# First block of x in four loads of two heads from two queues, in a fused attention and two-layer kernel

## The chip, the cores and the metric

The kernel runs on one core of a Trainium2 chip. The metric is the device time of one execution in microseconds. Engines: PE (TensorE), VectorE (DVE), ScalarE (ACT), GpSimd (POOL) and SyncE (SP). SP, ScalarE and POOL each issue DMAs to a queue of their own; the loads that change the type go through POOL's.

## The reference

```
x: (8, 8, 512, 64) f32 = B, H, S, D     state: (8, 8, 32, 64) f32
a     = softmax(x @ state^T / 8)        xread = a  @ state
a2    = softmax(state @ x^T / 8)        sread = a2 @ x
y     = concat([xread, sread], axis=2), heads side by side: (4352, 512)
h     = y @ w_in                        (512, 2048)
out   = (max(h, 0) + alpha * min(h, 0)) @ w_out      (2048, 512), out (4352, 512) f32
```

## The kernel before

The eight batches are blocks of 512 rows each; a ninth block holds the 256 rows of `sread`. `w_in` is applied to the states first (`state_w_in`, tiles `m`), so that a block's hidden rows come out of `m` and the softmax weights `aT` (`first`, step F, line 568). The ReLU-like function takes a ScalarE pass (`negative`, N) and a VectorE pass (`prelu`, G, line 624). The second layer is plain for block 0 (`second`, S, `second_out`, O) and uses sums and products of halves for the other blocks (U, P, K, Q).

The order of all work is written out by hand in the string `ORDER`: each token is a step with its arguments, and each engine runs its instructions in the order in which the tokens issue them. A letter `a`, `v` or `p` in a token names the engine (ScalarE, VectorE, POOL), a last digit on PE's steps the PSUM bank. The first tokens are

```
stc.0.a stt.0.1 sbd.0.a cx.0.0.v lst xt.0.0.0.2 cx.1.0.v sbd.1.a xt.0.1.0.3 xo.0.0.0.a tsc.0.0.4 xo.0.1.0.v tsc.1.0
cx.1.1.v Z.5.1 smax.0.0 xt.0.1.1.0 xo.0.1.1.v cx.0.1.a xt.0.0.1.2 ssh.v.0.0 sto.0.a Z.3.1 tsc.1.1.5 xo.0.0.1.a tsc.0.1
```

Before them stand the loads of x for block 0 (two, from SP's queue), of its states (64 KB, from ScalarE's queue), of alpha (four small ones, from SP's) and of the first part of `w_in` (POOL's), and nine filler matmuls (`fill`, Z, line 230) that keep PE going. Then:

- `stc` casts the first states (line 248), `stt` transposes them on PE (line 242), `sbd` copies them to `st_pairs` (line 262) and `sto` to `stT`.
- `cx.j.g` (`x0_cast`, line 175) casts to f16 one of two parts of x for the group `g` of four heads: before, all four heads, every other pair of rows (`j`).
- `xt.0.j.g` (`x_transposed`, line 300) transposes four 128x128 pieces of it on PE, `xo.0.j.g` (line 306) copies them to `xT`, `tsc.j.g` (`token_scores`, line 355) makes four score matmuls with `st_pairs`.
- `smax.0.g` (line 381), `ssh` (386), `sexp` (395), `ssum` (402, 403) and `snorm` (406) are the softmax of the first block in two halves, by group `g`; `at` and `ao` turn it into `aT`.
- `str`, `m`, `mo` prepare the other states and the tiles `m` (lines 242, 519, 543, 545).

The tile pool gives buffers by tag: the x tiles take the two of `ts` (4 KB a partition each), which the softmax tiles use afterwards. The tag `osb` has four of 2 KB, for rows of output.

Of the kernel before, what the change touches and what calls it, by code (L numbers as in the profile page):

```python
# [8 lines left out]
F32 = mybir.dt.float32  # L9
# [91 lines left out]
def kernel(  # L101
# [17 lines left out]
    nc = tc.nc  # L119

    B, H, S, D = x.shape
# [12 lines left out]
    att = ctx.enter_context(tc.tile_pool(name="att", bufs=2))  # L134
    moe = ctx.enter_context(tc.tile_pool(name="moe", bufs=2))
# [4 lines left out]
    def single(k, name, shape, dtype):  # L140
        return ps.tile(shape, dtype, name=name, tag=f"k{k}", bufs=1)
# [4 lines left out]
    def copier(e):  # L146
        return nc.scalar.copy if e == "a" else nc.vector.tensor_copy
# [4 lines left out]
    live = {}  # L152
    xgs = {}
    x0s = []
# [6 lines left out]
        )  # L161


    def load_x0(g):
        if g == 0:
            xgs["first"] = att.tile([128, H, 2, 2, D], F16, name="xg_first", tag="xg", bufs=3)
        t = att.tile([128, 4, 2, 2, D], F32, name=f"x0_{g}", tag="ts", bufs=2)
        x0s.append(t)
        nc.sync.dma_start(
            t.rearrange("p k j r d -> p k (j r d)"),  # L170
            x[0, 4 * g : 4 * g + 4].rearrange("k (p t) d -> p k (t d)", t=4),
        )

    def x0_cast(j, g, e):
        copier(e)(xgs["first"][:, 4 * g : 4 * g + 4, j, :, :], x0s[g][:, :, j, :, :])

    load_x0(0)
    load_x0(1)
    rows = state.rearrange("b h n d -> (b h n) d")
    n0 = H * N  # L180
    n_j = (B * H * N - n0) // 128
    st0_32 = consts.tile([128, 2, D], F32)
    nc.scalar.dma_start(st0_32, rows[:n0, :].rearrange("(g p) d -> p g d", p=128))
    alpha_rows = consts.tile([128, 32], F32)
    nc.vector.memset(alpha_rows, 0.0)
    alpha_quarters = moe_alpha.rearrange("(jc q c) -> q jc c", q=4, c=32)
# [28 lines left out]
    ident = consts.tile([128, 128], F16)  # L215
# [7 lines left out]
    st_pairs = consts.tile([128, H, 2, N], F16)  # L223
# [61 lines left out]
    def x_tile(b):  # L285
        if ("xT", b) not in live:
            live["xT", b] = att.tile([128, H, 2, 128], F16, name=f"xT_{b}", tag="xT", bufs=2)
        return live["xT", b]
# [7 lines left out]
    def x_transposed(b, j, g, k):  # L296
        b = b or "first"
        t = live["xp", b, j, g] = single(k, f"xT_ps{b}_{j}_{g}", [128, 4, 128], F16)
        for i in range(4):
            nc.tensor.transpose(  # L300
                t[:, i, :], xgs[b][:, 4 * g + i, j, :, :].rearrange("p r d -> p (r d)"), ident
            )

    def x_out(b, j, g, e):
        b = b or "first"
        copier(e)(x_tile(b)[:, 4 * g : 4 * g + 4, j, :], live.pop(("xp", b, j, g)))

    def scores(b, j=None):
        js = slice(0, 2) if j is None else slice(j, j + 1)
# [37 lines left out]
        soft_tiles(b)  # L347
        nc.vector.transpose(live["ts", b], live["sc", b].rearrange("p r j g s -> p (r j g s)"))

    def token_scores(j, g, k=None):  # L350
        if ("tsc", g) not in live:
            live["tsc", g] = single(k, f"tsc_{g}", [128, 2, 2, 4, N], F32)
        for k4 in range(4):
            h = 4 * g + (k4 ^ g)
            nc.tensor.matmul(
                live["tsc", g][:, j, :, k4, :],
                live["xT", "first"][:, h, j, :],
                st_pairs[:, h, :, :],
                start=True,
                stop=True,  # L360
                skip_group_check=True,
            )

    def tokens_transposed(j, k):
        t = live["at", j] = single(k, f"at_ps{j}", [128, 4, 128], F16)
# [386 lines left out]
    def quarter_out(b, th, dh, e=None):  # L752
# [12 lines left out]
        "stc": first_states_cast, "stt": first_states_transposed, "sto": first_states_out,  # L765
        "oma": one_less_alpha, "sbd": first_states_paired, "str": states_transposed, "sro": states_out,
        "xd": x_transposed_dma, "xt": x_transposed, "xo": x_out, "sc": scores, "cx": x0_cast, "tsc": token_scores,
        "at": tokens_transposed, "ao": tokens_out,
        "sb": score_blocks, "smax": state_max, "ssh": state_shift, "sexp": state_exp,
# [41 lines left out]
```

## Time and profile before

| | |
|---|---|
| median of 3 runs | 209.31 us (209.25 to 209.49) |
| profiled execution | 209.3 us, span of its instructions 207.2 us |
| PE busy | 198.9 us (96%) |
| VectorE busy | 182.6 us (88%) |
| ScalarE busy | 148.7 us (72%) |
| POOL busy | 144.0 us (70%) |
| granted TensorE clock | 1.000 |

Busy shares are means over the whole span. The start, the middle and the end of the kernel have different limits, so the stretch that a change touches is read by itself, in the timeline and in the chain of waits, which follows the work that ended last back to what released it.

### The profile page before, as it was taken

Reading aid. Unit: us, or ns where it says so; the run is one execution under the profiler, and the core shown is the slowest. Engines: PE = TensorE matmul, PEld = TensorE weight load, DVE = VectorE, ACT = ScalarE, POOL = GpSimd, SP = SyncE. Lnnn points to the kernel's source line nnn. Section 1 sums busy time; section 2 is a strip of 40 time slices with the busy share of each in tenths; the row PEclk is TensorE's granted clock in tenths of the full one; section 3 lists DMA queues with packets and bytes.
Section 4 is the critical chain, followed back from the end, with each engine's and each line's share of the span. In section 5 each row is a group of like instructions: output and inputs, shape, how many; then the busy total and the mean of one; then the engine's idle time right before and its main releaser. Section 6 shows DMA issues by size and latency. Waiting matters only on the chain.

```text
span 207.2 us, 5043 instructions
## 1 busy us (share of the span) xinstructions
PE 198.9 (96%) x2003; PEld 131.7 (64%) x2003; DVE 182.6 (88%) x277; ACT 148.7 (72%) x298; POOL 144.0 (70%) x87
## 2 busy tenths in 40 slices
PE   7789989999999999999999999999999999999992
PEld 2443433445666666677677766778767767888881
DVE  0899999999999999999999999998899988577650
ACT  3799998988789969988786899586677575321211
POOL 8173099999999999999897999949900697210100
PEclk9999999999999999999999999999999999999999
DMA  5999999949599999267979702112002021012134
GB/s 178 223 204 204 206 202 184 116 126 198 92 155 166 175 221 179 38 79 135 252 97 131 214 17 51 55 54 103 0 0 99 6 101 54 0 51 74 48 136 152
DMA packets 45943, 24.74 MB, mean 119 GB/s; under 512 B 24288, under 2 KB 45408, under 8 KB 45920
## 3 DMA queue, kind: packets, MB, share of 16 engines
q1 hardware_dynamic: 32960, 15.74, 31.2%
q0 software_dynamic: 12688, 8.62, 29.2%
q8 instruction: 15, 0.25, 0.5%
q10 hardware_dynamic: 272, 0.07, 0.1%
q14 instruction: 8, 0.07, 0.1%
HBM read 18.36 MB, written 8.91 MB: 132 GB/s over the span
## 4 chain that ended last, share of the span: by engine, by line
PE 81%; DVE 14%; issue 1%; DMA 1%; ACT 1%; POOL 0%; DVEq 0%; POOLq 0%; ACTq 0%
PE px L726 23%; PE h L568 23%; PE pv L726 12%; DVE g L624 7%; PE py L726 6%; PE o L638 6%; PE h L577 3%; PE m_ps L519 3%; PE fill L230 2%; DVE mx L381 1%; PE sr_ps L469 1%; DVE r L402 1%; DMA out_dram<-oq 1%; PE sc L316 1%; DVE ts L386 1%
## 5 line engine op out<-in xcount | busy, mean ns | idle before, releaser
L624 DVE SCALAR_TENSOR_TENSOR g<-neg,oma_sb,h 128x512 f16<-128x512 f32 (+1 forms) x144 | 94.5, 710 | 4.3 <-ACT neg L621 3.5
L621 ACT ACTIVATE neg<-h 128x512 f32<-128x512 f32 (+1 forms) x144 | 76.1, 590 | 14.0 <-PE h L568 8.2
L568 PE MATMUL h<-aT,m 128*128 128x512 f16 x256 | 64.5, 379 | 0.7 <-DVE g L624 0.5
L726 PEld LDWEIGHTS <-gsum 128*128 128x128 f16 x480 | 46.6, 98 | 9.6 <-issue 1.0
L568 PEld LDWEIGHTS <-m 128*128 128x128 f16 x256 | 24.1, 98 | 25.1 <-issue 4.3
L726 PEld LDWEIGHTS <-g 128*128 128x128 f16 x360 | 34.9, 98 | 7.3 <-issue 0.9
L705 POOL TENSOR_TENSOR gsum<-g 128x1024 f16<-128x1024 f16 (+1 forms) x14 | 28.7, 2060 | 14.4 <-PE pv L726 14.3
L705 POOL TENSOR_TENSOR gsum<-g,g 128x1024 f16<-128x1024 f16 x11 | 23.4, 2129 | 13.2 <-DVE g L624 13.1
L726 PE MATMUL px<-ws,gsum 128*128 128x256 f16 x240 | 29.8, 273 | 0.0
L742 ACT COPY kept<-px 128x512 f32<-128x512 f32 (+1 forms) x21 | 12.2, 582 | 23.8 <-PE px L726 22.8
L705 POOL TENSOR_TENSOR gsum<-gsum,g 128x1024 f16<-128x1024 f16 x11 | 23.4, 2126 | 3.4 <-DVE gsum L705 2.7
L705 POOL TENSOR_TENSOR gsum<-g,gsum 128x1024 f16<-128x1024 f16 x11 | 23.4, 2131 | 0.3
L545 ACT CAST m<-m_ps 128x512 f16<-128x512 f32 x36 | 19.9, 622 | 2.8 <-PE m_ps L519 2.7
L386 POOL TENSOR_TENSOR ts<-ts,mx 128x1024 f32<-128x1024 f32 x7 | 13.4, 1916 | 9.3 <-DVE mx L381 8.8
L638 PE MATMUL o<-w_out_sb,g 128*128 128x512 f16 x64 | 16.5, 379 | 0.0
L759 DVE TENSOR_TENSOR oq<-pv,kept 128x512 f32<-128x512 f32 (+1 forms) x16 | 10.5, 653 | 6.7 <-ACT kept L742 4.4
L726 PE MATMUL px<-w_out_sb,g 128*128 128x256 f16 x120 | 16.1, 273 | 0.0
L726 PE MATMUL px<-w_out_sb,gsum 128*128 128x256 f16 x120 | 16.1, 273 | 0.0
L726 PE MATMUL py<-w_out_sb,g 128*128 128x256 f16 x120 | 16.1, 273 | 0.0
L726 PE MATMUL pv<-ws,gsum 128*128 128x256 f16 x120 | 15.7, 273 | 0.0
L726 PE MATMUL pv<-ws,g 128*128 128x256 f16 x120 | 15.6, 273 | 0.0
L543 ACT CAST m<-m_ps 128x1024 f16<-128x1024 f32 x12 | 12.5, 1042 | 1.7 <-PE m_ps L519 1.6
(81 smaller groups left out, 232.7 us busy)
## 6 DMA issues: line engine op xcount, KB each, us to landing
out_dram<-oq SPq DMA_DIRECT2D x28, 256.0 KB, 2.6
xg<-in_x_dram POOLq DMA_DIRECT2D x8, 512.0 KB, 7.4
w_in_sb<-in_moe_w_in_dram POOLq DMA_DIRECT2D x4, 512.0 KB, 8.7
w_out_sb<-in_moe_w_out_dram POOLq DMA_DIRECT2D x4, 512.0 KB, 12.7
x<-in_x_dram SPq DMA_DIRECT2D x2, 512.0 KB, 4.9
out_dram<-osb SPq DMA_DIRECT2D x4, 256.0 KB, 4.3
out_dram<-oq SPq DMA_DIRECT2D x4, 128.0 KB, 2.1
st<-in_state_dram POOLq DMA_DIRECT2D x1, 224.0 KB, 7.3
```

Of the source, the lines that this page charges most:

```text
L386: engine(e).tensor_tensor(blocks(cols(live["ts", b], j, S)), blocks(scored(b, j)), over_blocks(cols(live["mx", b], j, S // N)), ALU.subtract,)
L519: nc.tensor.matmul(t[N * k : N * (k + 1), :], st_head(b, h)[64 * r : 64 * r + 64, :], w_in_sb[64 * r : 64 * r + 64, c, 512 * f : 512 * (f ...
L543: copier(e)(m_tile(b, f), t)
L545: copier(e)(m_tile(b, f)[:, g, :], t[g])
L568: nc.tensor.matmul(h.rearrange("p (r j s) -> p r j s", r=2, j=2), ms[b, f][:, g, 128 * j : 128 * (j + 1)], weights(b, g), start=(g == 0), ...
L621: nc.scalar.activation(neg, h, RELU, bias=0.0, scale=-1.0)
L624: nc.vector.scalar_tensor_tensor(g_tile(b, jc), negs.pop((b, jc)), oma_sb[:, jc : jc + 1], hs.pop((b, jc)), ALU.mult, ALU.add,)
L638: nc.tensor.matmul(outs[b, q], g_tile(b, jc)[:, 128 * q : 128 * (q + 1)], w_out_sb[:, jc, :], start=not begun and jc == 2 * jc2, stop=left ...
L705: engine(e).tensor_tensor(t, x(), y(), op)
L726: nc.tensor.matmul(pbanks[b, name][:, i, :], of(b, c)[:, j, 128 * i : 128 * (i + 1)], moving[:, 4 * c + j, :], start=not begun and j == 0, ...
L742: copier(e)(t, pbanks[b, "x"])
L759: nc.vector.tensor_tensor(osb, pbanks[b, name], kept[b, add], ALU.add)
```

## The change

Block 0 of x is loaded in four DMAs of two heads each (256 KB) instead of two of four heads (512 KB). Pairs 0 and 1 (heads 0 to 3) are issued from SP's queue, pairs 2 and 3 (heads 4 to 7) from ScalarE's, behind the first states. The steps keep their names, engines and places in `ORDER`, but their first number now picks a pair of heads of the group and not every other pair of rows: `cx.i.g` casts all rows of pair `i` of group `g`, `xt` transposes the four pieces of that pair, `xo` copies them, `tsc` makes its four score matmuls. The number and the size of casts, copies, transposes and matmuls stay the same. The tiles of the loads move from the tag `ts` to the tag `osb`.

```diff
-    def load_x0(g):
-        if g == 0:
+    def load_x0(pair, queue):
+        if pair == 0:
             xgs["first"] = att.tile([128, H, 2, 2, D], F16, name="xg_first", tag="xg", bufs=3)
-        t = att.tile([128, 4, 2, 2, D], F32, name=f"x0_{g}", tag="ts", bufs=2)
+        t = moe.tile([128, 2, 2, 2, D], F32, name=f"x0_{pair}", tag="osb", bufs=4)
         x0s.append(t)
-        nc.sync.dma_start(
+        queue.dma_start(
             t.rearrange("p k j r d -> p k (j r d)"),
-            x[0, 4 * g : 4 * g + 4].rearrange("k (p t) d -> p k (t d)", t=4),
+            x[0, 2 * pair : 2 * pair + 2].rearrange("k (p t) d -> p k (t d)", t=4),
         )
-    def x0_cast(j, g, e):
-        copier(e)(xgs["first"][:, 4 * g : 4 * g + 4, j, :, :], x0s[g][:, :, j, :, :])
-    load_x0(0)
-    load_x0(1)
+    def pair_of_heads(i, g):
+        return slice(4 * g + 2 * i, 4 * g + 2 * i + 2)
+    def x0_cast(i, g, e):
+        copier(e)(xgs["first"][:, pair_of_heads(i, g)], x0s[2 * g + i])
+    load_x0(0, nc.sync)
+    load_x0(1, nc.sync)
...
     nc.scalar.dma_start(st0_32, rows[:n0, :].rearrange("(g p) d -> p g d", p=128))
+    load_x0(2, nc.scalar)
+    load_x0(3, nc.scalar)
...
         for i in range(4):
-            nc.tensor.transpose(
-                t[:, i, :], xgs[b][:, 4 * g + i, j, :, :].rearrange("p r d -> p (r d)"), ident
-            )
+            if b == "first":
+                block = xgs[b][:, 4 * g + 2 * j + i // 2, i % 2, :, :]
+            else:
+                block = xgs[b][:, 4 * g + i, j, :, :]
+            nc.tensor.transpose(t[:, i, :], block.rearrange("p r d -> p (r d)"), ident)
...
-        copier(e)(x_tile(b)[:, 4 * g : 4 * g + 4, j, :], live.pop(("xp", b, j, g)))
+        t = live.pop(("xp", b, j, g))
+        if b == "first":
+            copier(e)(
+                x_tile(b)[:, pair_of_heads(j, g)].rearrange("p h j s -> p (h j) s"), t
+            )
+        else:
+            copier(e)(x_tile(b)[:, 4 * g : 4 * g + 4, j, :], t)
...
-    def token_scores(j, g, k=None):
+    def token_scores(i, g, k=None):
...
-        for k4 in range(4):
-            h = 4 * g + (k4 ^ g)
-            nc.tensor.matmul(
-                live["tsc", g][:, j, :, k4, :],
...
+        for h in range(8)[pair_of_heads(i, g)]:
+            for j in range(2):
+                nc.tensor.matmul(
+                    live["tsc", g][:, j, :, (h - 4 * g) ^ g, :],
```

More of the change, by code (lines that the diff above doesn't have):

```diff
@@ L348, in score_blocks @@
         nc.vector.transpose(live["ts", b], live["sc", b].rearrange("p r j g s -> p (r j g s)"))
-    def token_scores(j, g, k=None):
+    def token_scores(i, g, k=None):
         if ("tsc", g) not in live:
             live["tsc", g] = single(k, f"tsc_{g}", [128, 2, 2, 4, N], F32)
-        for k4 in range(4):
-            h = 4 * g + (k4 ^ g)
-            nc.tensor.matmul(
-                live["tsc", g][:, j, :, k4, :],
[L357 to L362, printed above, removed]
+        for h in range(8)[pair_of_heads(i, g)]:
+            for j in range(2):
+                nc.tensor.matmul(
+                    live["tsc", g][:, j, :, (h - 4 * g) ^ g, :],
+                    live["xT", "first"][:, h, j, :],
+                    st_pairs[:, h, :, :],
+                    start=True,
+                    stop=True,
+                    skip_group_check=True,
+                )
     def tokens_transposed(j, k):
```

## The prediction

> **What bounds the kernel now.** I began with the span and the clock, then busy time in three stretches (columns after the window: busy us of PE, PEld, DVE, ACT, POOL, then granted clock, DMA share, GB/s).
>
> ```profile
> core 0: 207.2 us, clock 1.000
> 7.70:15.60 7.90, 6.57 (x89) 3.46 (x89) 7.61 (x16) 6.78 (x13) 3.79 (x5) 1.00 1.25 205
> 15.60:30.00 14.40, 13.40 (x130) 5.58 (x129) 14.36 (x21) 14.38 (x28) 5.63 (x5) 1.00 1.31 204
> 30.00:200.00 170.00, 169.85 (x1730) 117.66 (x1729) 156.70 (x232) 122.83 (x251) 129.54 (x67) 1.00 0.52 103
> ```
>
> From 30 us on PE is busy 169.85 of 170.00 us: nothing in the change reaches that stretch, which only starts sooner or later. From 7.7 to 30 us VectorE is full (7.61 of 7.90, 14.36 of 14.40). The change lies ahead of that, so what it is worth is read at one instant: when VectorE begins its unbroken run. The chain of waits for the first 30 us says what sets that instant (start, length, what).
>
> ```profile
> 1.45 4.02 PE fill L230 x9
> 5.47 0.37 PE st_ps L242 x4
> 5.87 0.37 ACT st_pairs L262
> 6.25 0.37 ACT st_pairs L262
> 6.64 0.59 ACT xT_first L306
> 7.28 0.42 PE tsc L355 x8
> 7.72 0.69 DVE mx L381
> ```
>
> The run begins at 7.72 with the maximum over the first scores (step smax.0.0). Ahead of it stand nine filler matmuls, the transposes of the first states, three ScalarE copies in a row, and the scores. No cast of x and no landing of x is in this chain. The timeline of the first 13 us has the work around it (start, length, engine, line, what; in brackets the idle time before it and what ended it).
>
> ```profile
> 0.74 0.48 ACTq L183 DMA_DIRECT2D st<-in_state_dram  x1
> 0.74 1.02 SPq L169 DMA_DIRECT2D x<-in_x_dram  x2
> 1.25 1.28 ACT L248 ACT_TABLE_LOAD   x1 [1.25 <-PEq L795]
> 1.35 0.92 POOL L198 DMA_DIRECT2D w_in_sb<-in_moe_w_in_dram  x1
> 1.80 1.95 SPq L188 DMA_DIRECT2D alpha_rows<-in_moe_alpha_dram  x4
> 3.98 0.15 PEld L230 LDWEIGHTS <-pattern 128*128 128x128 f16 x1 [0.28 <-issue]
> 4.41 0.15 PEld L230 LDWEIGHTS <-pattern 128*128 128x128 f16 x1 [0.28 <-issue]
> 4.83 0.91 POOL L158 DMA_DIRECT2D xg<-in_x_dram  x1
> 4.88 0.30 ACT L248 CAST st<-st 128x128 f16<-128x128 f32 x1 [2.35 <-DMA st<-in_state_dram]
> 5.17 1.16 DVE L175 CAST xg_first<-x 128x512 f16<-128x512 f32 x2 [3.99 <-DMA x<-in_x_dram]
> 5.40 0.18 PEld L242 LDWEIGHTS <-st 128*64 128x64 f16 x4 [0.84 <-ACT st L248]
> 6.05 0.73 PE L300 MATMUL xT_psfirst<-ident,xg_first 128*128 128x128 f16 x8 [0.23 <-DVE xg_first L175]
> 6.81 0.42 DVE L306 COPY xT_first<-xT_psfirst 128x512 f16<-128x512 f16 x1 [0.49 <-PE xT_psfirst L300]
> 7.12 0.62 ACT L175 CAST xg_first<-x 128x512 f16<-128x512 f32 x1
> 7.16 0.42 DVE L175 CAST xg_first<-x 128x512 f16<-128x512 f32 x1
> 12.65 0.41 PE L519 MATMUL m_ps<-w_in_sb,stT 64*32 64x512 f16 x8 [0.79 <-DMA w_in_sb<-in_moe_w_in_dram]
> ```
>
> VectorE waits 3.99 us for x, but that is idle time before 7.72 that costs nothing: ScalarE's copy of the same half starts at 6.64, behind its two copies for st_pairs, when the transposed x has been there since about 6.5. Last, for the loads, the tile x (its casts and time from issue to landing), the line of the state's load, and DMA queues by window (packets, MB, share of 16 engines; q1 is SP's queue, q10 ScalarE's, q0 POOL's).
>
> ```profile
> L175 DVE CAST xg_first<-x x3: 407/417/828, 5.2 to 7.2; 128x512 f16<-128x512 f32 x3
> DMA to landing us min/median/max: 4.4/4.9/5.3
> DMA to landing us min/median/max: 4.1/4.1/4.1
> q1 hardware_dynamic: 444, 0.44, 73.7%
> q10 hardware_dynamic: 271, 0.07, 17.3%
> q1 hardware_dynamic: 269, 0.27, 109.5%
> q0 software_dynamic: 61, 0.06, 47.5%
> DMA packets 263, 0.21 MB, mean 206 GB/s; under 512 B 66, under 2 KB 263, under 8 KB 263
> q1 hardware_dynamic: 60, 0.12, 72.0%
> q0 software_dynamic: 66, 0.03, 48.8%
> ```
>
> The first landing row is x, the second the state. Then the windows: 2.7 to 4.4 us (q1, q10), 4.5 to 5.2 (q1, alone), 5.2 to 6 (q0's first packets), 6 to 7 (nearly all q0), 56 to 56.5 (q1 and q0 together). So x lands at 0.74+4.4 = 5.1 and at some 1.26+5.3 = 6.6, the state at 0.74+4.1 = 4.8. The second 512 KB takes 1.4 us, 0.7 us for 256 KB.
>
> **The change, part by part.**
>
> *When each pair lands.* The same 1 MB in the same 1 KB rows, so I keep the same total: the last pair lands when the last half does now, 6.6. Between, the queues share: from 2.7 to 4.4 us x and the state move side by side, 444 and 271 packets. Pair 0 has half the bytes of the present first load and lands first, 5.1-0.7 = 4.4. Pair 1 has two ends: 5.1, if pairs 2 and 3 take nothing from SP's queue, and 6.6, if all end together. I take it from the row of the state, which stands ahead of pair 2 on its queue: it lands 0.3 us before the first half of x; only from there on does pair 2 take turns, and pair 1's last 0.3 us doubles: 5.1+0.3 = 5.4. Pair 2 then follows at some 5.9, pair 3 at 6.6.
>
> *First half: casts, transposes, scores of heads 0 to 3.* The counts stay: four casts and four copies of 512 elements, 16 transposes, 16 score matmuls, at the durations above. VectorE casts pair 0 at 4.4 and pair 1 at 5.45. One cast took 828 ns against 407 to 417 for the others, at 5.17, inside POOL's DMA issue (4.83 to 5.74); so I charge 0.42 to 0.83 us, and pair 1 is cast by 5.9 to 6.3; now the second cast ends at 5.17+1.16 = 6.33. PE's transposes follow no later than now, and VectorE's copy stays at 6.81 or goes sooner. None of this moves smax.0.0, because ScalarE's copy still starts at 6.64 behind two copies that the change leaves alone. Worth: 0. The cover of pair 1 is about 0.45 us of landing (to 5.9); past that it costs one for one.
>
> *Second half.* VectorE's program has the cast of pair 3 (cx.1.1.v) ahead of smax.0.0, ScalarE's has pair 2 at 7.12. For no loss pair 3 must be in by 7.72-0.42-0.07 = 7.2; it lands at 6.6. Cover 0.6 us, worth 0. Behind this cast VectorE's whole run is queued, hence everything.
>
> *ScalarE's queue.* Two more issues at 0.48 us, ahead of the table load: it moves from 1.25 to about 2.27 and ends at 3.55. ScalarE idles 2.35 us before its cast at 4.88, so 1.3 us of cover are left: 0. The Trainium skill (ScalarE: Activation LUTs, What ACT_TABLE_LOAD costs) adds a drain of about 1.38 us to a table load of 1.28 us; no run here shows the drain, and by an estimate from it the cast would come at 4.93, 0.05 us later.
>
> *SP's queue.* The four alpha loads are issued as now. The last may come to wait for pair 0, if the two added loads use up the semaphores that loads take in turn: some 4.4 instead of 3.3 us; nothing stands behind it on SP but the transposing DMA of a later block, and alpha's reader on VectorE comes behind both halves of the first softmax. Cost 0.
>
> *Buffers.* The x tiles leave "ts" for "osb", whose next use is the first rows of output, once all first layers of a block are through. Nobody waits: 0.
>
> *The state's landing and PE's start.* Both x and state were issued at 0.74, and the state is one load of 64 KB beside 512 KB; now only 256 KB stand beside it. It may land up to 0.4 us sooner, or a little later with more loads open. Sooner helps little: fillers start 0.43 us apart (3.98, 4.41), so the nine leave PE free at 4.41+0.43+0.43 = 5.27, against 5.40 now. The chain gains 0 to 0.13 us; what is late next is the fill itself. I take -0.1, since ScalarE's cast is what ended PE's wait at 5.40. Later by 0.1 would cost 0.1.
>
> *Loads behind x.* POOL's first packets move after 5.2 us, as x runs out, although w_in was issued at 1.35; with the same bytes of x they begin as now, and PE's wait for w_in at 12.65 stays. That wait also caps a larger gain.
>
> Sum against the profiled execution, whose own time is 209.3 (span 207.2 and 2.1 around it): 207.2-0.1+2.1 = 209.2. The median of the runs is 209.31, so it is the same there.
>
> **The rivals.**
>
> *Pair 3 is overtaken by w_in (slower).* The last pair runs on ScalarE's queue after SP's x is done, a state that the trace does not have: now x alone holds the engines until the end (q1 alone from 4.5 to 5.2). If POOL's packets then take every second turn, 256 KB of w_in go between: at 206 GB/s (6 to 7 us) 1.25 us. Pair 3 lands at 7.85, its cast holds up smax.0.0 by 7.85-7.2 = 0.65 us: 209.9; with half of pair 2 caught too, 0.6 more: 210.5. It decides from a landing at 7.2. For it: from 56 to 56.5 us q1 and q0 do move 60 and 66 packets side by side, and in the row of 6 to 7 us 66 small packets (alpha's, on q1) ran between those of q0. Against: w_in got no packet while x ran. The Trainium skill (DMA: Bandwidth & Descriptors, Queues, rings and completion order) has every engine take turns between queues, packet by packet; the trace disagrees from 4.5 to 5.2 us and agrees at 56. Chance 0.27.
>
> *Pair 1 comes with the rest (slower).* All four move together, it lands at 6.6: cast to 7.1, transposes 0.4, copy 0.42, four scores 0.3 give 8.25 for smax.0.0, 0.5 later: 209.8. Against: the state ahead of pair 2. Chance 0.1.
>
> *The loads run faster (faster).* From 2 to 3.75 us the engines carry less than later:
>
> ```profile
> 2.00:3.75 1.75, 1.75 (x6) 0.61 (x5) 0.00 (x0) 0.53 (x1) 1.68 (x5) 1.00 0.71 212
> 3.75:5.50 1.75, 1.75 (x7) 0.40 (x6) 0.33 (x1) 0.30 (x1) 1.75 (x3) 1.00 1.09 378
> ```
>
> If two queues fill that gap, x is in (1-212/378)*1.75 = 0.8 us sooner, and w_in with it. The fill still holds PE to 5.27 and ScalarE's copies hold the rest, so 0.13 of it counts at 7.72; only if PE and ScalarE, with w_in sooner at 12.65, ran the stretch to 30 us better would 0.5 us come: 208.8. VectorE, full there, speaks against. Chance 0.13.
>
> *It does nothing at all:* 209.3, within the forecast.
>
> **How the numbers follow.** Forecast 0.5: 209.2, its own range 208.9 to 209.6. A measurement here tells about 0.2% from no change, 0.42 us: 208.9 to 209.7 counts as same. Faster 0.13 (the last rival, and a tail of the forecast: 0.15), slower 0.27+0.1 less what falls inside (0.36), same 0.49. The range for 8 in 10 reaches from 208.8 to 210.3: it holds the faster case's value and the overtaken pair 3 but for the far end.
>
> **What would show it.** Right: the chain of the first 30 us still goes fill, st_ps, two st_pairs copies, xT_first on ScalarE, tsc, mx, with mx at 7.6 to 7.75; x's first cast near 4.5; ScalarE's queue with three loads in a row and the table load near 2.3; q0's first packets after 5.2 us; busy times after 30 us unchanged. Wrong: an idle time of VectorE that ends with x before the cast in front of mx (pair 3), or PE's transposes in the chain with the cast of pair 1 behind them, or a state that lands well after 4.9 and moves st_ps past 5.47.

## The result and the profile after

The changed kernel takes 212.5 us in the median of 4 runs (211.51 to 212.94) against 209.36 us (209.25 to 209.49): slower by a ratio of 1.0141, 95% interval 1.0119 to 1.0162. The profiled execution took 212.8 us with a span of 210.9 us, 3.7 us more than before. The forecast was 209.2 us, the range 208.8 to 210.3: wrong.

The chain of waits, from the load that holds it to the second half's maximum (start, length, what; pieces called "issue", of 0.05 us at most, and a filler with eight scores are left out):

```profile
1.81 8.63 DMA x<-in_x_dram
10.47 0.44 DVE xg_first L178
10.95 1.02 PE xT_psfirst L309 x8
...
13.09 0.70 DVE mx L394
```

Where the filler matmuls and ScalarE's copies stood, there is now one load of x: 8.63 us from its issue at 1.81 to its landing at 10.44, then the cast, PE's transposes, a filler and eight scores, and the second half's maximum (smax.0.1) at 13.09. In the kernel before, that maximum is this line of the timeline:

```profile
9.35 0.69 DVE L381 TENSOR_REDUCE mx<-tsc 128x16 f32<-128x512 f32 x1
```

13.09-9.35 = 3.74 us, the span's 3.7 us. So the whole loss is made by 13.1 us, and none of it is given back afterwards. The timeline after:

```profile
0.74 0.49 ACTq L186 DMA_DIRECT2D st<-in_state_dram  x1
1.26 1.05 ACTq L169 DMA_DIRECT2D x<-in_x_dram  x2
2.33 1.28 ACT L253 ACT_TABLE_LOAD   x1 [2.33 <-issue]
1.77 2.55 SPq L193 DMA_DIRECT2D alpha_rows<-in_moe_alpha_dram  x4
3.85 0.53 DVE L178 CAST xg_first<-x 128x512 f16<-128x512 f32 x1 [2.67 <-DMA x<-in_x_dram]
4.01 0.30 ACT L253 CAST st<-st 128x128 f16<-128x128 f32 x1 [0.40 <-DMA st<-in_state_dram]
4.30 0.10 PEld L235 LDWEIGHTS <-pattern 128*128 128x128 f16 x1 [0.16 <-issue]
4.83 0.14 PEld L247 LDWEIGHTS <-st 128*64 128x64 f16 x4 [0.42 <-issue]
4.91 0.43 DVE L178 CAST xg_first<-x 128x512 f16<-128x512 f32 x1 [0.53 <-DMA x<-in_x_dram]
10.47 0.43 DVE L178 CAST xg_first<-x 128x512 f16<-128x512 f32 x1 [4.22 <-DMA x<-in_x_dram]
```

The first half did become earlier: pair 0 is cast at 3.85, pair 1 at 4.91, the state at 4.01, and PE begins with it at 4.83 instead of 5.40. Pair 3, the last cast, is the one that holds everything up: VectorE waits 4.22 us for it. The DMA queues say what ran meanwhile (2.7 to 4.4 us, two rows; 4.4 to 5.2 us, two rows; 5.2 to 7.7 us, two rows; 7.7 to 10.4 us, two rows; packets, MB, share of 16 engines; alpha's small packets left out):

```profile
q1 hardware_dynamic: 410, 0.39, 67.6%
q10 hardware_dynamic: 405, 0.21, 41.4%
q0 software_dynamic: 82, 0.08, 69.5%
q10 hardware_dynamic: 138, 0.12, 46.2%
q0 software_dynamic: 319, 0.33, 79.3%
q10 hardware_dynamic: 221, 0.21, 32.2%
q0 software_dynamic: 453, 0.53, 113.4%
q10 hardware_dynamic: 39, 0.04, 4.9%
```

Until 4.4 us x and the state had the engines to themselves. From then on POOL's queue (w_in) runs beside ScalarE's: 82 packets by 5.2 us, in a stretch (4.5 to 5.2 us) in which the kernel before moved x alone. From 5.2 us about as many packets are left on ScalarE's queue as pair 3 has, and the last 39 take 2.7 us. The trace has 16 completion signals for each load of x, and a load has landed with the last of them. Of pair 3's, twelve had come by 7.99 us; the last four came at 9.18, 9.28, 9.44 and 10.45. In the kernel before, all 16 of either load came within 0.81 us. Busy time by window shows what the wait does to PE (columns as in the prediction):

```profile
7.70:10.40 2.70, 0.00 (x0) 0.00 (x0) 0.00 (x0) 0.00 (x0) 0.00 (x0) 1.00 1.20 209
12.00:13.00 1.00, 0.96 (x16) 0.62 (x15) 0.61 (x2) 0.94 (x2) 0.00 (x0) 0.50 1.25 209
30.00:200.00 170.00, 169.31 (x1709) 115.63 (x1708) 158.16 (x232) 126.67 (x259) 133.33 (x68) 1.00 0.52 103
```

PE, VectorE, ScalarE and POOL stand still for 2.7 us; after that the granted clock is 0.50 from 12 to 13 us, and the step from the cast's start to the second maximum takes 13.09-10.47 = 2.62 us instead of 9.35-7.16 = 2.19: 0.43 us of the loss. The other 3.31 us are the cast itself, 10.47 against 7.16. From 30 us on PE is nearly as full as before (169.31 of 170.00 us, 169.85 before).

### The profile page after: what moved, and what is told of

Same layout as the page of the kernel before. It is cut to its first block, busy times and chain, and to the rows that moved or that the text cites. A ratio compares the mean times of both kernels' runs of the same rounds, so it can differ in the third digit from the quotient of the medians.

```text
span 210.9 us, 5046 instructions
## 1 busy us (share of the span) xinstructions
PE 199.5 (95%) x2003; PEld 132.3 (63%) x2003; DVE 182.5 (87%) x277; ACT 148.9 (71%) x298; POOL 144.1 (68%) x87
## 4 chain that ended last, share of the span: by engine, by line
PE 75%; DVE 15%; DMA 5%; issue 2%; ACTq 1%; ACT 0%; DVEq 0%
PE px L739 22%; PE h L581 21%; PE pv L739 11%; DVE g L637 8%; PE py L739 6%; PE o L651 5%; DMA x<-in_x_dram 4%; PE h L590 3%; PE m_ps L532 3%; DVE ts L361 1%; DVE r L415 1%; PE sr_ps L482 1%; DMA out_dram<-oq 1%; PE sc L329 1%; DVE mx L394 1%
## 5 line engine op out<-in xcount | busy, mean ns | idle before, releaser
L718 POOL TENSOR_TENSOR gsum<-g,g 128x1024 f16<-128x1024 f16 x11 | 23.5, 2132 | 13.2 <-DVE g L637 13.1
L772 DVE TENSOR_TENSOR oq<-pv,kept 128x512 f32<-128x512 f32 (+1 forms) x16 | 10.4, 653 | 6.7 <-ACT kept L755 4.4
## 6 DMA issues: line engine op xcount, KB each, us to landing
w_out_sb<-in_moe_w_out_dram POOLq DMA_DIRECT2D x4, 512.0 KB, 10.5
```

What stands on the lines that cost most here:

```text
L718: engine(e).tensor_tensor(t, x(), y(), op)
L772: nc.vector.tensor_tensor(osb, pbanks[b, name], kept[b, add], ALU.add)
```

## The experiments

Theories at the start: A, w_in is held off by SyncE's queue but not by ScalarE's; B, the time of issue decides: loads issued early go ahead of w_in on any queue, one issued from about 1.8 us on takes turns with it; C, the smaller pieces cost by themselves, as loads or as steps. D, formed later: a fourth load is late whatever w_in does. Line numbers shift with each edit; the names stay.

**All four loads from SyncE's queue.**

```diff
-    load_x0(2, nc.scalar)
-    load_x0(3, nc.scalar)
+    load_x0(2, nc.sync)
+    load_x0(3, nc.sync)
```

> All four loads of pairs from SyncE's queue, the rest as in the changed kernel. Theory A (POOL's w_in waits for SyncE's queue but takes turns with ScalarE's): all pairs are in by 6.6 us, the maximum at 7.0 to 7.7, 208.5 to 209.3 us. Theory B (what is issued early goes first whatever the queue, what is issued from some 1.8 us on takes turns with w_in): pairs 2 and 3, issued near 1.75 and 2.25, land at 8 to 11 us, 212 us or more. Theory C (the smaller pieces themselves cost it): 212 to 213 us.

Measured: 213.34 us, ratio 1.0187 (1.0171 to 1.0203). Its x tile (the issues, the time to landing):

```profile
L169 SPq DMA_DIRECT2D x<-in_x_dram x4: 446/469/472, 0.7 to 2.3; - x4
DMA to landing us min/median/max: 3.0/4.4/8.9
```

and the last cast in VectorE's timeline:

```profile
11.23 0.43 DVE L178 CAST xg_first<-x 128x512 f16<-128x512 f32 x1 [4.90 <-DMA x<-in_x_dram]
```

On SyncE's queue too the last pair, issued at 2.28, lands 8.9 us later. Theory A falls: SyncE's queue is no protection.

**The kernel before, its second load on ScalarE's queue.**

```diff
...
-    load_x0(0)
-    load_x0(1)
+    load_x0(0, nc.sync)
...
+    load_x0(1, nc.scalar)      # behind the state's load
```

> The kernel before, with only its second load of four heads moved to ScalarE's queue behind the state (issued near 1.26 us). Theory A: it takes turns with w_in and lands at 9 to 11 us, 212 us or more. Theory B: issued as early as pair 2 was, it goes ahead of w_in and lands by 6.6, 209.0 to 209.4 us. Theory C: 209.3.

Measured: 209.19 us, ratio 0.9989 (0.9978 to 1.0): no loss. The load, issued near 1.3 us, lands 5.5 us later:

```profile
DMA to landing us min/median/max: 4.6/5.0/5.5
```

ScalarE's queue does no harm to a load that is issued early.

**Casts and scores by pairs, the loads of before.**

```diff
...
-        copier(e)(xgs["first"][:, pair_of_heads(i, g)], x0s[2 * g + i])
-
-    load_x0(0, nc.sync)
-    load_x0(1, nc.sync)
+        copier(e)(xgs["first"][:, pair_of_heads(i, g)], x0s[g][:, 2 * i : 2 * i + 2])
+
+    load_x0(0)      # four heads, SyncE
+    load_x0(1)
...
-    load_x0(2, nc.scalar)
-    load_x0(3, nc.scalar)
```

> Casts, transposes, copies and scores by pairs as in the changed kernel, but x in the two loads of four heads from SyncE's queue of the kernel before. Theories A and B: 209.0 to 209.5 us, the loads are the whole loss. Theory C: 212 to 213 us.

Measured: 209.4 us, ratio 1.0012 (0.9995 to 1.0029). The compute by pairs costs nothing that shows: theory C falls for the steps. For the loads it falls with the next runs, where four small loads come on time.

**w_in held back by six patterns of POOL's work.**

```diff
+    for _ in range(6):
+        nc.gpsimd.iota(w_out_sb[:, 0, :], pattern=[[19, 512]], ...)
     load_w_in(0)
     ident = consts.tile([128, 128], F16)
```

> The changed kernel with 3.4 us of POOL's own work (six more number patterns, written where w_out comes later) ahead of its first load, so that w_in starts after x. Theories A and B: pair 3 lands before 6.5, the first maximum comes at about 7.1, w_in is 0.3 us later than in the kernel before; 208.8 to 209.9 us. Theory C, or a ScalarE queue that is slow by itself: pair 3 late again, 212 us or more.

Measured: 211.25 us, ratio 1.0093 (1.0078 to 1.0108), outside what either side expected. The first load of w_in, and with it all of POOL's loads, is issued at 5.25 us, 3.9 us later than in the changed kernel and not the 3.4 that the expectation counted. The x tile:

```profile
DMA to landing us min/median/max: 3.0/3.8/4.2
```

PE's timeline:

```profile
6.80 0.43 PE L252 MATMUL st_ps<-ident,st 128*64 128x128 f16 x4 [1.32 <-POOL ident masks.py:199]
```

Every load of x now lands within 4.2 us, so POOL's loads, w_in first, are what made the fourth late. The time is lost elsewhere: the identity, also POOL's work, came behind the added patterns, and PE waited for it until 6.80. PE's next eight transposes took 1.03 us, against 0.73 before, so its slower pace has a part too. The run settles the landing, not the time; the next runs put the identity first.

**w_in issued a little later: 1.86 us and 3.00 us instead of 1.35.**

```diff
-    load_w_in(0)
     ident = consts.tile([128, 128], F16)
     make_identity(nc, ident)
+    for _ in range(2):          # in the second of the two runs only
+        nc.gpsimd.iota(w_out_sb[:, 0, :], pattern=[[19, 512]], ...)
+    load_w_in(0)
```

> The changed kernel with POOL's identity made ahead of the first load of w_in, whose issue moves from 1.35 to about 1.95 us. Theory B: the last pair, issued at 1.79, is now level with w_in or ahead of it, lands by 7 us, 208.5 to 209.5 us; if the lead is too short, half of the loss stays (210.5). Theory D (the fourth load is late whatever w_in does): 212 to 213 us.

> As the run before, and two more number patterns (1.1 us of POOL's work) between the identity and the first load of w_in, issued near 3.1 us. Theory B: the last pair lands by 6.2 us, the first maximum at 7.0 to 7.2; w_in starts as x runs out, no later than 5.3, so its readers do not wait longer: 208.4 to 209.0 us. Theory D: 212 to 213 us.

Measured: issued at 1.86, 210.39 us, ratio 1.005 (1.0026 to 1.0073), with a wide scatter (209.13 to 211.63), and the last pair 7.5 us from issue to landing in the profile, which is that of the slowest of the ten runs; issued at 3.00, 208.99 us, ratio 0.9983 (0.9971 to 0.9995), a little faster than the kernel before. The second run's x tile:

```profile
DMA to landing us min/median/max: 3.0/3.8/4.2
```

Its DMA queues from 4.5 to 5.7 us:

```profile
q10 hardware_dynamic: 348, 0.33, 77.6%
q0 software_dynamic: 42, 0.04, 32.2%
```

Its timeline:

```profile
6.29 0.80 DVE L178 CAST xg_first<-x 128x512 f16<-128x512 f32 x1
7.22 0.69 DVE L399 TENSOR_REDUCE mx<-tsc 128x16 f32<-128x512 f32 x1
12.32 0.41 PE L537 MATMUL m_ps<-w_in_sb,stT 64*32 64x512 f16 x8 [0.80 <-DMA w_in_sb<-in_moe_w_in_dram]
```

POOL's 42 packets come as x runs out, pair 3 waits for nobody at 6.29, the first maximum is at 7.22 (7.72 before), and PE gets w_in at 12.32, not later than before (12.65), although it was issued 1.65 us later. Holding w_in back removes the whole loss in two steps: the fourth load is on time when w_in is issued late enough, and D falls. Two things stay open. In the first of the two runs pair 3, issued near 1.8, was about as far ahead of w_in (1.86) as the second load was in the kernel before (1.28 against 1.35), and still was late: theory B is right that the time of issue matters, but its plain form, first issued goes first, doesn't cover this run, and how much of a lead is needed is not shown. And not all of the earlier maximum need be the edit's: in this profile the nine fillers took 3.64 us, against 4.02 before, so that PE came to the state at 5.02. What that is worth in the 208.99 us is not separated.

**Three loads, the last issued early.**

```diff
...
-    load_x0(2, nc.scalar)
-    load_x0(3, nc.scalar)
+    load_x0(4, 4, nc.scalar)      # heads 4 to 7 in one load of 512 KB
```

> Pairs 0 and 1 from SyncE's queue as in the changed kernel, heads 4 to 7 in one load of 512 KB from ScalarE's queue, so that the last load of x is issued near 1.26 us and not at 1.8. Theory B (what is issued early goes ahead of w_in): everything is in by 6.6 us, the state and the first maximum stay early (7.0 to 7.2), 208.5 to 209.1 us. If the number of loads or their order on ScalarE's queue is what matters (theory D), the half load takes turns with w_in, lands at 9 or later: 211.5 us or more.

Measured: 208.95 us, ratio 0.9994 (0.9981 to 1.0007). The slowest landing is 4.8 us after issue; no loss, and the interval does not tell it from the kernel before. The x tile:

```profile
DMA to landing us min/median/max: 3.2/4.6/4.8
```

The timeline:

```profile
5.40 0.18 PEld L250 LDWEIGHTS <-st 128*64 128x64 f16 x4 [0.83 <-issue]
7.73 0.69 DVE L397 TENSOR_REDUCE mx<-tsc 128x16 f32<-128x512 f32 x1
```

Here the state was cast at 3.46 and PE still came to it at 5.40, after "issue", its own filler matmuls: an early state alone brings nothing.

**The converse: the kernel before, its second load 0.5 us later.**

```diff
     load_x0(0)
-    load_x0(1)
...
         nc.sync.dma_start(alpha_rows[32 * q : 32 * q + n_jc, :], alpha_quarters[q])
+        if q == 0:
+            load_x0(1)
```

> The kernel before, its two loads of four heads from SyncE's queue and all its steps, with only one small alpha load issued between them, so that the second load is issued 0.5 us later, near 1.8 us. Theory B (time of issue against w_in decides, not the queue, the number or the size of the pieces): the second half takes turns with w_in and lands at 9 to 11 us, 212 us or more. If pairs or the number of loads matter: 209.2 to 209.6 us.

Measured: 212.9 us, ratio 1.0163 (1.0139 to 1.0186). Queue, size, number and steps are those of the kernel before; only the second load's issue moved from 1.28 to 1.81. SyncE's and VectorE's timeline:

```profile
0.74 0.47 SPq L169 DMA_DIRECT2D x<-in_x_dram  x1
1.28 0.48 SPq L187 DMA_DIRECT2D alpha_rows<-in_moe_alpha_dram  x1
1.81 0.42 SPq L169 DMA_DIRECT2D x<-in_x_dram  x1
10.42 0.43 DVE L175 CAST xg_first<-x 128x512 f16<-128x512 f32 x1 [3.16 <-DMA x<-in_x_dram]
```

The x tile, and behind it the queues from 5.2 to 10.4 us:

```profile
DMA to landing us min/median/max: 4.2/6.4/8.6
```

```profile
q0 software_dynamic: 784, 0.86, 97.1%
q1 hardware_dynamic: 389, 0.29, 23.2%
```

The same landing, 8.6 us after issue, the same cast at 10.42, the same loss: half a microsecond of issue is enough for the whole effect. (A small load of alpha now stands ahead of the late load on its queue; in the changed kernel none does, and pair 3 is as late.)

**Filling PE's wait.**

```diff
-cx.1.1.v Z.5.1 smax.0.0
+cx.1.1.v Z.5.15 smax.0.0
```

> The changed kernel with fifteen filler matmuls instead of one where PE waits for pair 3 (3.2 us at full clock). If the lower granted clock after the wait (0.5 from 12 to 14 us) is a part of the loss, PE's transposes and scores after the wait take 0.6 to 0.7 us less in sum: 211.5 to 212.1 us. If the clock costs nothing, because VectorE or ScalarE set the pace there: 212.3 to 212.9 us.

Measured: 213.67 us, ratio 1.0227 (1.019 to 1.0265), above both expectations. In the profiled execution, the fastest of the four (212.19), pair 3 was cast at 7.95, and PE was held by its own fillers until 10.76: there the run costs what it was meant to save, and its time says nothing on the clock. Its PE lines do: at full clock the eight transposes behind the fillers take 0.61 us, against 1.02 in the chain of the changed kernel above, and the way from their start to the second maximum takes 12.38-10.76 = 1.62 us, against 13.09-10.95 = 2.14. So the lower clock is a part of the loss.

```profile
10.76 0.61 PE L309 MATMUL xT_psfirst<-ident,xg_first 128*128 128x128 f16 x8
12.38 0.69 DVE L394 TENSOR_REDUCE mx<-tsc 128x16 f32<-128x512 f32 x1 [0.17 <-PE tsc L368]
```

**The first maximum ahead of pair 3's cast.**

```diff
-cx.1.1.v Z.5.1 smax.0.0 xt.0.1.1.0 xo.0.1.1.v cx.0.1.a xt.0.0.1.2 ssh.v.0.0
+Z.5.1 smax.0.0 ssh.v.0.0 cx.1.1.v xt.0.1.1.0 xo.0.1.1.v cx.0.1.a xt.0.0.1.2
```

> The changed kernel with VectorE's first maximum and first subtraction (smax.0.0, ssh.v.0.0) moved in the order ahead of the cast of pair 3. Theory V (as predicted: that cast in front of smax.0.0 is what makes the late pair cost, since all of VectorE's run is queued behind it): the run starts at 7.0 again and 1.4 us or more come back, 211 us or less. Theory S (the second half's own chain, cast, PE, copy, scores, second maximum, is the later one anyway): 0 to 0.3 us, 212.2 to 212.8 us in the median, with the spread of the changed kernel.

Measured: 213.91 us, ratio 1.0207 (1.0173 to 1.0242), above both expectations; nothing came back. VectorE's timeline, in the slowest of the four runs (214.61), where pair 3 landed later still:

```profile
7.73 0.69 DVE L394 TENSOR_REDUCE mx<-tsc 128x16 f32<-128x512 f32 x1 [0.68 <-PE tsc L368]
12.32 0.43 DVE L178 CAST xg_first<-x 128x512 f16<-128x512 f32 x1 [3.18 <-DMA x<-in_x_dram]
14.95 0.69 DVE L394 TENSOR_REDUCE mx<-tsc 128x16 f32<-128x512 f32 x1 [1.07 <-PE tsc L368]
```

The first maximum is done at 7.73, and the second still comes 14.95-12.32 = 2.63 us after the cast, as without the edit (2.62). Theory S holds for the mechanism, though not for the time: the second half's own chain sets the end.

**Seven fillers at the start.**

```diff
-    fill(0, 9)
+    fill(0, 7)        # in the kernel with w_in issued at 3.00
```

> The kernel with w_in issued near 3.1 us (208.99 us), with seven filler matmuls at the start instead of nine. If the fillers hold PE while the state is already cast at 4.25 us (that cast was at 3.96 to 4.26 there, and PE came at 5.02), PE's first transposes come 0.4 to 0.8 us sooner and the first maximum at 6.6 to 7.0: 208.3 to 208.8 us. If two fillers less leave PE at its lower pace for longer, or pair 1 and the w_in landing set the pace next: 208.9 to 209.6 us.

Measured: 209.29 us, ratio 0.9997 (0.9982 to 1.0012): no gain over nine.

```profile
4.55 0.42 PE L252 MATMUL st_ps<-ident,st 128*64 128x128 f16 x4
7.01 0.67 DVE L399 TENSOR_REDUCE mx<-tsc 128x16 f32<-128x512 f32 x1
12.73 0.41 PE L537 MATMUL m_ps<-w_in_sb,stT 64*32 64x512 f16 x8 [0.87 <-DMA w_in_sb<-in_moe_w_in_dram]
13.51 0.76 DVE L388 COPY aT<-at_ps 128x512 f16<-128x512 f16 x2 [0.62 <-PE at_ps L385]
```

PE and the first maximum come sooner (4.55, 7.01), but w_in lands no sooner (PE waits for it until 12.73, with nine fillers until 12.32), PE's next transposes queue behind it, and VectorE idles 0.62 us at 13.5.

## Why the prediction was wrong, point by point

- **"When each pair lands" is the step that failed**, for pair 3: forecast 6.6, measured 1.81+8.63 = 10.44. It kept the landing of the last byte because the bytes were the same, and the order of issue was not looked at: the second load of x moved from about 1.28 to a last pair near 1.8, behind POOL's w_in at 1.35. The converse run shows that this half microsecond is enough. The row on which I leaned, x alone on the engines from 4.5 to 5.2 us with w_in long issued, is no right of x over w_in: with the last load of x issued near 1.8, w_in's packets ran from about 4.4 us in the profile. For the same reason "Loads behind x" failed, which had w_in begin after 5.2 as now.
- **The rival that named it** (0.27) had the right mechanism and a price of 0.65 to 1.25 us against 3.7. One term is mis-sized: 1.25 us for 256 KB of w_in between. Most of pair 3 did land so: 221 packets from 5.2 to 7.7, and twelve of its 16 completion signals by 7.99. But a load has landed only with its last part, and the last 39 packets and four signals took until 10.4. The Trainium skill (DMA: Bandwidth & Descriptors, Queues, rings and completion order) has the engines take turns between queues packet by packet; from 5.2 us on the trace agrees in so far as both queues move side by side (319 packets of POOL's beside 221). Why an early load is let through whole, and why a few parts of a late one fall so far behind, no run here shows.
- **"Second half"**: its deadline of 7.2 us was right in kind, the way of the loss wrong. Not the cast in front of smax.0.0 but the cast, PE, copy and scores of the second half set the run; taking smax.0.0 out of the queue gave nothing.
- **The lower clock after the wait** was in no step. It is the 0.43 us by which the way from the cast to the second maximum grew: PE's part took 2.14 us instead of 9.35-7.74 = 1.61, less 0.10 us by which PE, with nothing else to do, began sooner after the cast.
- **Pairs 0 and 1**: forecast 4.4 and 5.4, measured casts at 3.85 and 4.91. Right in sign. ScalarE's queue: table load forecast at 2.27, measured 2.33, harmless. The Trainium skill (ScalarE: Activation LUTs, What ACT_TABLE_LOAD costs) adds a drain of some 1.38 us to it; the trace disagrees, the cast came 0.40 us after the load's end, released by the state. SP's queue: alpha's issues stretch from 1.95 to 2.55 us, as allowed, and stand nowhere in the chain. Compute by pairs: worth 0, as forecast.
- **The state and PE's start**: PE came 0.57 us sooner, not 0 to 0.13, but only because the last filler matmuls ran closer together there (the one at 4.30, 0.43 us apart before). The trace's first record of the full clock is at 4.18 us, in the kernel before at 5.92. With an equally early state and no such quickening (three loads, first record at 6.14) PE came at 5.40. That w_in caps a gain from there was right: the run with seven fillers shows it.

## What to carry to other kernels

In this start, loads that share the DMA engines were served roughly in the order of their issue, over all queues, but a lead of less than 0.1 us was enough in one kernel and not in another. Moving a load 0.5 us back can put it beside another engine's bulk load, and its last parts then land microseconds late. When a load is split, write down the issue time of each piece next to the issue of every other load in flight, and price the last piece with turns taken, as the least that it can cost: here that came to 1.25 us, and the piece landed 3.8 us late. If a split is wanted, hold the bulk load back instead: with w_in issued 1.65 us later this change loses nothing and measured a little faster than before (0.9983, 0.9971 to 0.9995), and w_in's readers lose nothing.

## What the runs showed of the hardware

The last 256 KB of x, issued near 1.8 us, took 4.2 us from issue to landing where w_in was issued at 3.00 us or later, and 6.2 to 10.5 us where it was issued at 1.35 or 1.86 (6.2 with the added fillers, 7.5 with the identity first, 8.6 in the changed kernel, 10.5 with the maximum first). From profile to profile of the same loads the cast behind them came at 7.95, 10.47 and 12.32.

The granted clock fell to 0.50 at 11.0 us in the changed kernel, 3.8 us after PE's last matmul, but at 9.63, 1.7 us after it, in the run with the maximum first. At 0.50 eight transposes took 1.02 us instead of 0.61.

A granted clock of 1.00 at the start of a window table is not a measurement where the trace has no record yet: the kernel before has its first at 5.92 us, and until then its fillers stand 0.43 us apart, against 0.23 for those added in the changed kernel later on (fifteen in 3.40 us). The converse run has its first record at 14.15 us, and its eight transposes behind the wait took 1.03 us, though the window table prints 1.00 there.
